# A wait on VectorE for GpSimd's next planned instruction, in an attention and mixture kernel

## The chip, the cores and the metric

The kernel runs on one core of a Trainium2 chip. The metric is the device time of one execution in microseconds (us). The engines are TensorE (PE in the rows; PEld is its weight load), VectorE (DVE), ScalarE (ACT), GpSimd (POOL) and SyncE (SP), which issues the DMAs.

## What is computed

Two stages, both over batch 4, sequence 768. The first is attention over 8 heads of 64 in which a query sees only keys of its own hash bucket (six signs of a projection); the second takes its output (4 x 768 x 512) as the input of a mixture of four causal attention experts, two of which are chosen for each row.

```
q_bits = (q @ proj > 0); k_bits = (k @ proj > 0)          # 6 bits -> bucket
scores = where(q_bucket == k_bucket, scale * q @ k^T, -1e9)
x = softmax(scores) @ v                                   # 8 heads -> 512 columns
logits = x @ w_gate; the two largest of 4 -> softmax -> w
for e in 4 experts:
    q, k, v = x @ wq[e], x @ wk[e], x @ wv[e]
    a = softmax(causal(scale * q @ k^T))
    out += w[e] * (a @ v @ wo[e])
```

## The kernel before

**Units.** The work is cut into 48 units: for each batch 8 heads of the first stage ("L") and 4 experts of the second ("M"). A unit first has a pass for its row maxima (matmuls into `mx`, reduced by VectorE into `pm`), then scores in chunks of up to 512 columns (matmuls into `st`, three PSUM buffers), and for each chunk two exponentials on ScalarE: `p` in float32 and `ph` in float16. GpSimd subtracts them: `pl = p - ph` is the low half, so that a product with float32 precision is made of float16 matmuls. `pl` has five buffers, `p` four. TensorE then adds three matmuls for each 128 columns into `o`: `vh,ph`, `vl,ph` and `vh,pl`. Some chunks are kept whole in float32 (`pf`, matmul `o<-vf,pf`). `vl` is the low half of v, made by GpSimd from `vf` and `vh` too.

**Preparing a pair of heads** (`prep_pair`). For two heads at a time `natq` and `natk` (float32, 128 x 768) are loaded, ScalarE makes the scaled float16 half (`qk<-natq,cs`), and VectorE the rest: `scalar_tensor_tensor` `qk<-natq,cs,qk`, an instruction that reads two SBUF operands. There are 14 such for q and 14 for k. Then follow projection matmuls into `misc`, the signs `M`, and DMAs (`qk<-M`, `qk<-qk`) that lay the rows out. In the last unit VectorE also takes five of the `pl` subtractions, the other instructions of it with two SBUF operands that last long.

**The order.** Nothing is issued as it is written. A recorder keeps every operation, and `schedule()` plans: from a table of durations (`TIMES`) and priorities (`prio`, with the table `PLACE`) it picks, step by step, the operation that can start first on any engine, and `issue()` emits them in that order. Each engine then runs its own list strictly in order, and waits on semaphores for what it reads or overwrites. For the planner, `port` marks VectorE's instructions with two SBUF operands; `hold` is the planned start and end of the last of these, `grain` the planned start and end of GpSimd's last instruction. The planner knows that the two do not overlap: a marked VectorE instruction that starts in the middle of a GpSimd one is given an end after it, and a GpSimd instruction planned within `hold` starts 130 ns before its end. But this is only arithmetic for the order. In the program nothing ties the two engines together there: which of them goes first is settled when it runs. All instructions are emitted by one line, so rows carry L711 throughout and are told apart by their tiles.

Of the kernel before, what the change touches and what calls it, by code (L numbers as in the profile page):

```python
# [42 lines left out]
class View:  # L43
# [42 lines left out]
    def real(self):  # L86
        x = self.tile.real
        for name, args, kw in self.path:
            x = getattr(x, name)(*args, **kw)
        return x  # L90
# [42 lines left out]

class Op:
    __slots__ = ("i", "alts", "ins", "outs", "preds", "succ", "wait", "ready", "new", "done", "prio", "wide", "dma",
                 "bias", "end", "eng", "tag", "job")


PRIO = {"norm": -300, "pair_scales": -100, "shift_steps": -100, "halves": 50, "mixture_scales": -3000, "weights": 400}
# [325 lines left out]
class Recorder:  # L465
# [102 lines left out]
    def schedule(self):  # L568
        groups = {}
        for o in self.ops:  # L570
            g = groups.setdefault((str(o.job), o.alts[0][0]), len(groups))
            o.prio = o.i + PRIO.get(o.tag, 0) + PRIO.get((o.tag, o.alts[0][0]), 0) + (PLACE[g] if PLACE else 0)
            o.wait, o.done, o.eng = len(o.preds), False, None
            for p in o.preds:
                p.succ.append(o)
        free = dict(START)
        cand = {e: [] for e in free}

        def sources(o, e):
            other = {p if p.eng == "sync" else p.eng for p in o.preds if p.eng != e}  # L580
            return len(other) > 1

        def after(p, e, many):
            if p.eng == e:
                return p.end + SAME[e]
            return p.end + (LAT_PE[e] if e in LAT_PE and many and p.eng == "tensor" else (LAT2 if many else LAT)[e])

        def enter(o):
            o.ready = {}
            for a in o.alts:  # L590
                e, r = a[0], 0.0
                many = sources(o, e)
                for p, over in o.preds.items():
                    if p.eng == e and (e == "tensor" or not over):
                        continue
                    r = max(r, after(p, e, many))
                o.ready[e] = r
                cand[e].append((o, a))

        for o in self.ops:  # L600
            if not o.wait:
                enter(o)
        order = []
        last = queue = 0.0
        grain = hold = (-1e9, -1e9)
        left = len(self.ops)
        while left:
            left -= 1
            best = None
            for e, lst in cand.items():  # L610
                t0 = free[e]
                k0 = k1 = 1e18
                pick = None
                for o, a in lst:
                    r = o.ready[e]
                    if max(t0, r) > k0:
                        continue
                    ok = True
                    for i, c in enumerate(o.new):
                        if not c.placed:  # L620
                            old = c.ring.ready(c, sum(d.ring is c.ring for d in o.new[:i]))
                            if old is None:
                                ok = False
                                break
                            if old:
                                for p in old.ops:
                                    if p.eng != e or e != "tensor":
                                        r = max(r, after(p, e, False))
                    if not ok:
                        continue  # L630
                    st = max(t0, r)
                    pen = max(0.0, 107.0 - last - max(0.0, st - t0)) if e == "tensor" and o.wide else 0.0
                    if a[4][4] and grain[1] > st + 187.0 and grain[0] + 80.0 < st:
                        pen = grain[1] - 187.0 - st
                    if len(o.alts) > 1 and a is o.alts[1]:
                        f = o.alts[0]
                        late = free[f[0]] + sum(p.alts[0][4][0] for p, _ in cand[f[0]] if p.prio < o.prio and p.ready[f[0]] <= st)
                        if max(late, r) + f[4][1] <= st + pen + a[4][1] - o.bias:
                            continue
                    k = st + pen  # L640
                    if k < k0 or (k == k0 and o.prio < k1):
                        k0, k1, pick = k, o.prio, (st, o, a, pen)
                if pick and (best is None or pick[0] < best[0]):
                    best = pick
            if best is None:
                raise RuntimeError("no instruction can go")
            st, o, a, pen = best
            e = a[0]
            busy, lasts, lands, shares, port = a[4]
            for x in o.alts:  # L650
                cand[x[0]] = [y for y in cand[x[0]] if y[0] is not o]
            if e == "tensor":
                st += pen if o.wide else 0.0
                last = busy
                if st < COLD and busy < 300:
                    busy *= 1.85
                if self.filler and self.filler[0].done:
                    gap = st - max(free[e], self.filler[2])
                    if any(c.name == "o" for c in o.new):
                        self.filler = None  # L660
                    elif st < FILL_END:
                        for _ in range(int(0.8 * (gap - FILL_GAP) / (107.0 if st < COLD else 55.0))):
                            order.append((self.filler[0], self.filler[1]))
            if o.dma is not None:
                free[e] = st + busy
                o.end = max(st + lasts + lands, queue + shares)
                queue = max(queue, o.end)
                o.end += LATE
            elif e == "gpsimd":
                if hold[1] - 130.0 > st and hold[0] < st + 80.0:  # L670
                    st = hold[1] - 130.0
                grain = (st, st + lasts)
                free[e], o.end = st + busy, st + lasts
            elif port:
                o.end = st + lasts
                if grain[1] > st + 187.0 and grain[0] + 80.0 < st:
                    o.end = max(o.end, grain[1] + lasts - 187.0)
                free[e] = o.end - (lasts - busy)
                hold = (st, o.end)
            else:  # L680
                free[e], o.end = st + busy, st + lasts
            o.eng = e
            for c in o.new:
                if not c.placed:
                    c.placed = True
                    c.ring.done.append(c)
                    c.ring.next += 1
            for c in {x.tile for x in o.ins + o.outs}:
                c.left -= 1
            o.done = True  # L690
            if self.filler and o is self.filler[0]:
                self.filler = (o, self.filler[1], o.end + 300.0)
            for p in o.succ:
                p.wait -= 1
                if not p.wait:
                    enter(p)
            order.append((o, a))
        self.length = max(o.end for o in self.ops)
        return order

    def issue(self):
        def real(x):
            if not isinstance(x, View):
                return x
            return x.real()

        for o, (e, m, args, kw, _) in self.schedule():
            for c in o.new:
                if c.real is None:
                    c.real = c.pool.tile(c.shape, c.dtype, name=c.name, bufs=c.bufs)  # L710
            getattr(getattr(self.nc, e), m)(*[real(x) for x in args], **{k: real(x) for k, x in kw.items()})  # L711

# [30 lines left out]
@with_exitstack  # L745
def tile_kernel(ctx, tc, q, k, v, proj, w_gate, wq, wk, wv, wo, out):
    nc = Recorder(tc.nc, loose=("misc",))
    B, HP, _, _, HS = q.shape
    E, Dm, D = wq.shape
    H, S = 2 * HP, 2 * HS  # L750
# [82 lines left out]
    for j in range(2):  # L833
        part = slice(D * j, D * j + D)
        for sign, c0, n in ((1.0, 32 * j, 70), (-1.0, 32 * j + NB, 58)):
            x = first[part, c0:c0 + 2 * n].rearrange("p (a b) -> p a b", a=2)[:, :, 0:NB]
# [4 lines left out]
    for g in range(4):  # L841
        o = 32 * g
# [19 lines left out]
    for j in range(2):  # L862
        part = slice(D * j, D * j + D)
        for sign, lo, hi in ((1.0, 0, 88), (-1.0, 2 * NB, 2 * NB + 40)):
            x = signed[part, lo:hi].rearrange("p (a b) -> p a b", a=2)[:, :, j:j + 2 * NB:2]
# [1019 lines left out]
```

## Time and profile before

| | us |
|---|---|
| median of 3 runs | 617.88 |
| lowest, highest | 616.58, 618.98 |
| the profiled execution, its own time | 618.62 |
| its span, first to last instruction | 616.8 |
| PE busy | 596.4 (97%) |
| DVE busy | 505.8 (82%) |
| ACT busy | 502.1 (81%) |
| POOL busy | 466.9 (76%) |
| mean granted TensorE clock | 0.986 |

Busy time counts an instruction from its start to its end as the profiler saw them, so an instruction that has started and stands still counts as busy. Matmuls overlap, so PE's share is of time in which at least one is under way. A granted clock of 1.00 is the 2.4 GHz level and 0.50 the 1.2 GHz level. In a row of the timeline the two numbers are start and duration in us; xN are N instructions in a row; the bracket is how long the engine had been idle before, and what ended that.

### The profile page before, as it was taken

What the parts mean: (1) busy time and instruction counts of PE and PEld (TensorE: products, weight loads), DVE (VectorE), ACT (ScalarE), POOL (GpSimd) and SP (SyncE); (2) the same over time, 40 slices, a digit from 0 to 9 for tenths busy, and PEclk for the clock granted to TensorE, in tenths of its full rate; (3) what the DMA queues carried; (4) which work ended last, traced back from release to release, by engine and by line L of the source; (5) the groups of instructions that cost most, each with busy time, mean ns of one, the idle gap of its engine ahead of it and who ended that gap; (6) DMA issues with size and microseconds to landing.
All of it is one profiled execution on the core that took longest, in us unless ns stands there. A gap on an engine that the chain in (4) does not pass through costs nothing.

```text
span 616.8 us, 20449 instructions
## 1 busy us (share of the span) xinstructions
PE 596.4 (97%) x7850; PEld 431.7 (70%) x7850; DVE 505.8 (82%) x1374; ACT 502.1 (81%) x1075; POOL 466.9 (76%) x520
## 2 busy tenths in 40 slices
PE   8999996999999999999999999999999999999997
PEld 6668874767677776777776666767766767777673
DVE  5897888899999899988989879895979884557753
ACT  6686995899979889886998798896987978953784
POOL 9476795799976889995897679886895878961640
PEclk9997997999999999999999999999999999999999
DMA  6552072233242113232233314132024121001222
GB/s 183 168 143 66 12 194 95 55 96 64 77 146 91 47 29 112 52 96 63 73 85 120 106 54 124 39 105 59 16 92 126 51 51 29 24 20 42 63 86 103
DMA packets 38967, 50.24 MB, mean 81 GB/s; under 512 B 13226, under 2 KB 27350, under 8 KB 38870
## 3 DMA queue, kind: packets, MB, share of 16 engines
q1 hardware_dynamic: 38870, 48.95, 27.9%
q8 instruction: 61, 1.00, 0.7%
q14 instruction: 36, 0.29, 0.2%
HBM read 20.98 MB, written 6.29 MB: 44 GB/s over the span
## 4 chain that ended last, share of the span: by engine, by line
PE 77%; DVE 9%; ACT 7%; POOL 2%; issue 2%; DMA 1%; SPq 1%; ACTq 0%; DVEq 0%; POOLq 0%
PE st L711 24%; PE misc L711 22%; PE o L711 19%; PE mx L711 12%; DVE qk L711 3%; DVE pm L711 3%; ACT ph L711 2%; ACT p L711 2%; DVE misc L711 1%; ACT wst L711 1%; SPq L711 1%; POOL qk L711 1%; ACT qk L711 1%; DMA wst<-in_moe_wk_dram 0%; DMA xt<-roww 0%
## 5 line engine op out<-in xcount | busy, mean ns | idle before, releaser
L711 POOL TENSOR_TENSOR pl<-p,ph 128x512 f16<-128x512 f32 x367 | 411.4, 1148 | 120.7 <-ACT ph L711 57.8
L711 ACT ACTIVATE p<-st 128x512 f32<-128x512 f32 x372 | 230.1, 623 | 32.0 <-PE st L711 25.8
L711 ACT ACTIVATE ph<-st 128x512 f16<-128x512 f32 x372 | 230.4, 629 | 1.0 <-PE o L711 0.8
L711 PE MATMUL st<-qk 78*128 78x512 f16 (+3 forms) x976 | 229.8, 326 | 0.9 <-DMA qk<-row 0.6
L711 DVE TENSOR_REDUCE pm<-mx 128x2 f32<-128x512 f32 (+2 forms) x284 | 186.9, 675 | 18.0 <-PE mx L711 16.7
L711 PEld LDWEIGHTS <-ph 128*128 128x128 f16 x2880 | 157.5, 98 | 26.1 <-issue 1.8
L711 PEld LDWEIGHTS <-qk 128*128 128x128 f16 (+5 forms) x1560 | 130.6, 98 | 58.3 <-issue 8.8
L711 PE MATMUL mx<-qk 76*128 76x512 f16 (+2 forms) x488 | 137.0, 328 | 7.1 <-DVE pm L711 6.4
L711 PEld LDWEIGHTS <-pl 128*128 128x128 f16 x1440 | 132.8, 97 | 7.8 <-POOL pl L711 1.7
L711 PE MATMUL o<-vh,ph 128*128 128x65 f16 (+1 forms) x1104 | 127.1, 195 | 2.4 <-DVE xp L711 0.9
L711 PE MATMUL o<-vl,ph 128*128 128x64 f16 x1104 | 126.6, 193 | 0.2 <-POOL vl L711 0.2
L711 PE MATMUL o<-vh,pl 128*128 128x65 f16 (+1 forms) x1104 | 125.4, 194 | 0.0
L711 PE MATMUL misc<-xt,wqk_h 128*128 128x384 f16 x256 | 57.7, 325 | 0.2 <-DVE qk L711 0.2
L711 DVE CUSTOM_DVE_ANT_0 spare<-mx,causal 128x512 bf16<-128x512 f32 (+2 forms) x96 | 44.3, 461 | 9.2 <-PE mx L711 7.4
L711 PEld LDWEIGHTS <-xt 128*128 128x128 f16 x324 | 30.3, 97 | 10.8 <-ACT xt L711 0.5
L711 PE MATMUL o<-mvh,pl 128*128 128x65 f16 x336 | 37.2, 193 | 0.6 <-POOL pl L711 0.6
L711 PE MATMUL o<-mvh,ph 128*128 128x65 f16 x336 | 37.5, 194 | 0.0
L711 PE MATMUL o<-mvl,ph 128*128 128x64 f16 x336 | 37.4, 192 | 0.0
L711 POOL TENSOR_TENSOR vl<-vf,vh 128x384 f16<-128x384 f32 x32 | 30.6, 967 | 7.8 <-ACT vh L711 7.8
L711 PEld LDWEIGHTS <-wqk_h 128*128 128x128 f16 x256 | 24.1, 98 | 14.6 <-issue 0.3
L711 ACT ACTIVATE qk<-misc 128x384 f16<-128x384 f32 x26 | 13.2, 507 | 20.3 <-PE misc L711 20.1
L711 PE MATMUL misc<-wvg_h,xt 128*128 128x260 f16 x192 | 29.7, 274 | 0.0
(198 smaller groups left out, 911.3 us busy)
## 6 DMA issues: line engine op xcount, KB each, us to landing
qk<-qk SPq DMA_DIRECT2D x128, 96.0 KB
natv<-in_v_dram SPq DMA_DIRECT2D x16, 384.0 KB
qk<-qk SPq DMA_DIRECT2D x32, 192.0 KB
natq<-in_q_dram SPq DMA_DIRECT2D x15, 384.0 KB
natk<-in_k_dram SPq DMA_DIRECT2D x15, 384.0 KB
out_dram<-ot SPq DMA_DIRECT2D x20, 256.0 KB
xt<-xt SPq DMA_DIRECT2D x4, 192.0 KB
out_dram<-p SPq DMA_DIRECT2D x3, 256.0 KB
```

Source lines behind the costliest of these rows:

```text
L711: getattr(getattr(self.nc, e), m)(*[real(x) for x in args], **{k: real(x) for k, x in kw.items()})
```

## The change

In the planner, each VectorE instruction with two SBUF operands that lasts 400 ns or more by the table is remembered (`half`). The next GpSimd instruction whose planned start lies more than 100 ns after that instruction's start gets it as `after`, and when it is emitted a semaphore wait on that VectorE instruction is added to it. If a second such VectorE instruction is planned before any GpSimd instruction qualifies, it takes the place of the first, so that one wait stands for both. The plan's times, the ranks and so the order are not touched.

```diff
@@ schedule()
-            o.wait, o.done, o.eng = len(o.preds), False, None
+            o.wait, o.done, o.eng, o.after = len(o.preds), False, None, None
...
         grain = hold = (-1e9, -1e9)
+        half = None
...
             elif e == "gpsimd":
+                if half is not None and hold[0] + 100.0 < st:
+                    o.after, half = half, None
                 if hold[1] - 130.0 > st and hold[0] < st + 80.0:
                     st = hold[1] - 130.0
...
                 hold = (st, o.end)
+                if lasts >= 400.0:
+                    half = o
...
@@ issue()
-            getattr(getattr(self.nc, e), m)(*[real(x) for x in args], **{k: real(x) for k, x in kw.items()})
+            o.made = getattr(getattr(self.nc, e), m)(*[real(x) for x in args], **{k: real(x) for k, x in kw.items()})
+            if o.after is not None:
+                self.tc.add_manual_dep(o.made.ins, o.after.made.ins.name,
+                                       mybir.DependencyInfo(mybir.DependencyClass.Sync, mybir.DependencyReason.DATA), reason="port")
@@ tile_kernel()
     nc = Recorder(tc.nc, loose=("misc",))
+    nc.tc = tc
```

The program has 33 VectorE instructions that are remembered (28 `qk` and 5 `pl`) and gets 25 waits, all on GpSimd: 18 on `pl` of the units before the last, 5 on `vl`, 1 on `wvg_l` (a weight's low half) and 1 on the `pl` that GpSimd keeps in the last unit. The lists of TensorE, VectorE, ScalarE and SyncE are the same as before, word for word.

The first place is the third of the 14 pairs that are prepared this way, 94 us into the span. VectorE's list there, before and now (the two `qk` residuals stand one behind the other, so one wait serves both, and it is on the second):

```order
L711 TENSOR_REDUCE qkmax<-wst 128x2 [waits DMAHW3_49,DMAHW0_49]
L711 TENSOR_TENSOR xp<-o,rden 128x6x64 [waits DVE_49]
L711 TENSOR_REDUCE qkmax<-wst 128x2 [waits DMAHW2_49,DMAHW1_49]
L711 SCALAR_TENSOR_TENSOR qk<-natq,cs_1846,qk 128x2x384 [waits Activation_49]
L711 SCALAR_TENSOR_TENSOR qk<-natk,cs_1846,qk 128x2x384 [waits Activation_49,Pool_49]
L711 TENSOR_REDUCE pm_177<-mx 128x2 x2
L711 TENSOR_REDUCE qkmax<-wst 128x2 [waits DMAHW5_49,DMAHW4_49]
```

Nothing moved in it: the reductions `pm` that free the two `mx` buffers for TensorE are queued behind both residuals (`qkmax` is the largest entry of a weight in `wst`). GpSimd's list at 94 us, before (numbers behind `p` are buffer names):

```order
L711 TENSOR_TENSOR pl<-p_1949,ph 128x512 [waits PE_49,Activation_49,Pool_49]
L711 TENSOR_TENSOR pl<-p_1981,ph 128x512 [waits PE_49,Activation_49,Pool_49]
L711 TENSOR_TENSOR vl_939<-vf_259,vh_253 128x6x64 x2
L711 TENSOR_TENSOR pl<-p_2054,ph 128x512 [waits PE_49,Activation_49,Pool_49]
L711 TENSOR_TENSOR pl<-p_2094,ph 128x512 [waits PE_49,Activation_49,Pool_49]
L711 TENSOR_TENSOR pl<-p_2111,ph 128x512 [waits PE_49,Activation_49,Pool_49]
```

and with the change:

```order
L716 TENSOR_TENSOR pl<-p_1949,ph 128x512 [waits PE_49,Activation_49,Pool_49]
L716 TENSOR_TENSOR pl<-p_1981,ph 128x512 [waits PE_49,Activation_49,Pool_49]
L716 TENSOR_TENSOR vl_939<-vf_259,vh_253 128x6x64 x2
L716 TENSOR_TENSOR pl<-p_2054,ph 128x512 [waits PE_49,DVE_49,Activation_49,Pool_49]
L716 TENSOR_TENSOR pl<-p_2094,ph 128x512 [waits PE_49,Activation_49,Pool_49]
L716 TENSOR_TENSOR pl<-p_2111,ph 128x512 [waits PE_49,Activation_49,Pool_49]
```

No row has moved; the first `pl` behind the two `vl` has one more semaphore to wait for, VectorE's, and what is queued behind it on GpSimd waits with it. The second place is the pair at 332 us, on GpSimd before:

```order
L711 TENSOR_TENSOR vl_939<-vf_259,vh_253 128x6x64 [waits Activation_49]
L711 TENSOR_TENSOR pl<-p_7524,ph 128x256 [waits PE_49,Pool_49]
L711 TENSOR_TENSOR pl<-p_7657,ph 128x512 [waits PE_49,Activation_49,Pool_49]
L711 TENSOR_TENSOR pl<-p_7685,ph 128x512 [waits PE_49,Activation_49,Pool_49]
L711 TENSOR_TENSOR pl<-p_7757,ph 128x512 [waits PE_49,Activation_49,Pool_49]
```

and with the change:

```order
L716 TENSOR_TENSOR vl_939<-vf_259,vh_253 128x6x64 [waits DVE_49]
L716 TENSOR_TENSOR pl<-p_7524,ph 128x256 [waits DVE_49,PE_49,Pool_49]
L716 TENSOR_TENSOR pl<-p_7657,ph 128x512 [waits PE_49,Activation_49,Pool_49]
L716 TENSOR_TENSOR pl<-p_7685,ph 128x512 [waits PE_49,Activation_49,Pool_49]
L716 TENSOR_TENSOR pl<-p_7757,ph 128x512 [waits PE_49,Activation_49,Pool_49]
```

Here the second `vl` waits for the residual of q and the `pl` behind it for that of k: two waits on two instructions that follow each other.

## Rows read from the trace of the kernel before

**Rows 1.** The page: busy time of each engine; the chain by engine.

```profile
PE 596.4 (97%) x7850; PEld 431.7 (70%) x7850; DVE 505.8 (82%) x1374; ACT 502.1 (81%) x1075; POOL 466.9 (76%) x520
...
PE 77%; DVE 9%; ACT 7%; POOL 2%; issue 2%; DMA 1%; SPq 1%; ACTq 0%; DVEq 0%; POOLq 0%
```

**Rows 2.** Timeline of PE, 90 to 112 us: start, duration, instruction, idle before.

```profile
96.25 0.33 PE L711 MATMUL misc<-qk,pbl 128*32 128x384 f16 x3
101.56 0.59 PE L711 MATMUL mx<-qk 76*128 76x512 f16 x1 [4.97 <-DVE pm L711]
...
107.35 0.24 PE L711 MATMUL o<-vh,pl 128*128 128x65 f16 x1
```

**Rows 3.** Timeline of DVE, 90 to 108 us.

```profile
93.93 6.04 DVE L711 SCALAR_TENSOR_TENSOR qk<-natq,cs,qk 128x768 f16<-128x768 f32 x1
99.89 1.00 DVE L711 SCALAR_TENSOR_TENSOR qk<-natk,cs,qk 128x768 f16<-128x768 f32 x1
100.82 1.28 DVE L711 TENSOR_REDUCE pm<-mx 128x2 f32<-128x512 f32 x2
```

**Rows 4.** Timeline of POOL, 75 to 108 us.

```profile
74.71 4.12 POOL L711 TENSOR_TENSOR pl<-p,ph 128x512 f16<-128x512 f32 x3
...
92.88 1.83 POOL L711 TENSOR_TENSOR vl<-vf,vh 128x384 f16<-128x384 f32 x2
94.66 4.50 POOL L711 TENSOR_TENSOR pl<-p,ph 128x512 f16<-128x512 f32 x4
104.01 0.92 POOL L711 TENSOR_TENSOR vl<-vf,vh 128x384 f16<-128x384 f32 x1 [4.86 <-ACT vh L711]
```

**Rows 5.** Stretches: length; busy PE, PEld, DVE, ACT, POOL; granted clock; DMA.

```profile
85.00:95.00 10.00, 9.12 (x137) 7.01 (x134) 9.78 (x27) 9.64 (x20) 10.00 (x11) 1.00 0.76 169
95.00:100.60 5.60, 1.58 (x33) 1.03 (x32) 5.60 (x2) 2.34 (x6) 4.15 (x4) 1.00 0.62 214
100.60:110.80 10.20, 9.24 (x55) 5.55 (x55) 7.75 (x13) 4.66 (x10) 3.19 (x3) 0.50 0.11 27
...
110.80:122.00 11.20, 10.91 (x182) 8.73 (x181) 9.58 (x34) 11.05 (x23) 8.78 (x8) 1.00 0.20 46
```

**Rows 6.** Timeline of ACT, 88 to 112 us.

```profile
102.39 0.27 ACT L711 ACTIVATE vr<-misc 1x128 f16<-1x128 f32 x1 [5.05 <-PE misc L711]
...
103.41 0.53 ACT L711 ACTIVATE vh<-vf 128x384 f16<-128x384 f32 x1
105.76 0.62 ACT L711 ACTIVATE vf<-natv,cs 128x384 f32<-128x384 f32 x1 [1.83 <-PE o L711]
...
110.12 0.60 ACT L711 ACTIVATE p<-st 128x512 f32<-128x512 f32 x1 [1.79 <-PE st L711]
```

**Rows 7.** Tile natq: the residuals of q; least, median, most ns.

```profile
L711 DVE SCALAR_TENSOR_TENSOR qk<-natq,cs,qk x14: 996/1015/6045, 35.2 to 480.6; 128x768 f16<-128x768 f32 x14
```

**Rows 8.** Timeline of DVE at four other residuals.

```profile
75.57 1.11 DVE L711 SCALAR_TENSOR_TENSOR qk<-natk,cs,qk 128x768 f16<-128x768 f32 x1
...
155.29 2.14 DVE L711 SCALAR_TENSOR_TENSOR qk<-natq,cs,qk 128x768 f16<-128x768 f32 x1 [0.57 <-ACT qk L711]
...
196.87 1.76 DVE L711 SCALAR_TENSOR_TENSOR qk<-natk,cs,qk 128x768 f16<-128x768 f32 x1
...
331.81 2.14 DVE L711 SCALAR_TENSOR_TENSOR qk<-natq,cs,qk 128x768 f16<-128x768 f32 x1
```

**Rows 9.** Tile pl: the subtraction on POOL; who waited for it (us, times).

```profile
L711 POOL TENSOR_TENSOR pl<-p,ph x367: 664/1155/1882, 22.1 to 601.7; 128x512 f16<-128x512 f32 x169, 128x384 f16<-128x384 f32 x15
...
  PEld L711: 1.7, 6
```

**Rows 10.** Timeline of PE: its idle time behind three of those residuals.

```profile
159.60 0.38 PE L711 MATMUL mx<-qk 76*128 76x512 f16 x1 [0.26 <-DVE pm L711]
...
199.64 0.23 PE L711 MATMUL misc<-identh,negh 128*128 128x128 f16 x1 [0.58 <-DVE negh L711]
...
337.86 0.23 PE L711 MATMUL misc<-identh,negh 128*128 128x128 f16 x1 [0.66 <-DVE negh L711]
```

More of the change, by code (lines that the diff above doesn't have):

```diff
@@ L135 @@
     __slots__ = ("i", "alts", "ins", "outs", "preds", "succ", "wait", "ready", "new", "done", "prio", "wide", "dma",
-                 "bias", "end", "eng", "tag", "job")
+                 "bias", "end", "eng", "tag", "job", "after", "made")
 PRIO = {"norm": -300, "pair_scales": -100, "shift_steps": -100, "halves": 50, "mixture_scales": -3000, "weights": 400}
```

## The prediction

> **What bounds the kernel now.** I read the page first, then PE's idle time, then what stood before it on the other engines. By the page PE has work under way for 97% of the span and is most of the chain [rows 1]: there is little idle time to win, so the question is where the little is, and what the clock did there. Of PE's idle pieces one stands out: 4.97 us, ended by VectorE's `pm`, before the matmul into `mx` at 101.56 us [rows 2]. The last instruction before it started at 96.25 (a row of three, so PE went idle at 101.56 - 4.97 = 96.6).
>
> VectorE was not idle. The residual of q started at 93.93 and took 6.04 us, that of k followed at 99.89, and the `pm` behind them came only at 100.82 [rows 3]. The same residual takes 1.015 us in the median of its 14 calls, and 6.045 at most [rows 7]. So about 5.0 us of the 6.04 are standing still. What it stood still for is seen on GpSimd: at 93.93 it was in the second of two `vl`, and then ran four `pl` without a gap, up to 94.66 + 4.50 = 99.16 [rows 4]. The residual ended 0.81 us after that, when GpSimd had nothing more to run. Both read two operands from SBUF; the residual stood through the rest of that `vl` and was passed over by four `pl` in a row.
>
> The stretch after it shows a second cost. From 100.6 to 110.8 PE is busy for 9.24 of 10.20 us at a granted clock of 0.50, the 1.2 GHz level; in the stretches before and after it is 1.00 [rows 5]. PE had been idle for 4 us, from 96.6, when it fell. That is the place where this change has something to win.
>
> **The change part by part.**
>
> *The wait at 94 us.* The first `pl` behind the two `vl` now waits for the residual of k. GpSimd can then get no further than the second `vl`, which ends at 92.88 + 1.83 = 94.71 [rows 4]. The residual of q runs from about there and ends near 95.6, that of k 0.93 later (the steps of [rows 3]: 100.82 - 99.89) near 96.5, and the first `pm`, half of a row of two that takes 1.28, some 0.6 later at 97.1. Before, this was at 101.5. PE resumes 4.45 us earlier, and 0.5 us of its idle time stays.
>
> *The clock.* With an idle piece of 0.5 us I expect 1.00 to stay: from 85 to 95 us PE was busy for 9.12 of 10.00, so idle for 0.9, and the clock held [rows 5]. PE's 9.24 us at half speed would then need 4.62 at the least, 4.62 less. PE alone therefore allows 4.45 + 4.62 = 9.05 us.
>
> *Who is next.* ACT is busy for 11.05 of 11.20 us in the stretch after that [rows 5], so no more comes through than ACT loses of its idle time. That was 5.05 + 1.83 + 1.79 = 8.67 us [rows 6]. Scaled: `vr` starts 0.83 us after PE resumes (102.39 - 101.56), at full clock 0.42, so near 97.5, where ACT had been free since 102.39 - 5.05 = 97.34: 0.2 us stays. `vf` at 105.76 came 4.2 after PE, so 2.1 now, and ACT is through `vh` (103.41 + 0.53) about as late: 0.2 stays. Before 110.12 nothing stays, since PE halves its 8.56 us and ACT's own work of 2.56 does not shrink. ACT allows 8.2. VectorE: 4.4 earlier at the end of the residuals, and its idle time from 100.6 to 122 is 2.45 + 1.62 = 4.07 [rows 5], 8.5 together, of which it must win nearly all. Three engines near their limit don't all win all of it. I take 7.5 for this place, nearest to ACT, with 4.45 (clock stays low, or other engines eat it) and 9.05 as ends.
>
> *The other waits.* Three more residuals lost a turn or more to GpSimd: 2.14, 1.76 and 2.14 us [rows 8] against 1.01; with the wait they would be through some 0.6 to 0.9 earlier (one `wvg_l`, one `vl` that comes after). PE stood idle behind them for 0.26, 0.58 and 0.66 [rows 10], 1.5 in all; half of it is my estimate, 0.7.
>
> *What the waits cost on GpSimd.* At 94 us the `pl` starts when the residual of k has ended and been seen, 96.5 + 0.07 (the handover from ACT's `vh`, 103.94, to `vl` at 104.01 [rows 4, 6]) instead of 94.66: 1.9 us of idle time on an engine that was busy for 10.00 of 10.00 us before [rows 5]. Behind it are three more `pl`. What covers it: the first of them is used at 107.35 [rows 2], 11.5 us after its end at 95.8; even with PE 9 us earlier that is 2.5 of margin against 1.9. At the three other lost turns the guarded instruction comes about 1 us later. At nine waits GpSimd's instruction was already standing and started as VectorE let go (the longest `pl`, 1882 ns against a median of 1155 [rows 9]); to see one: the three `pl` from 74.71 end at 78.83 [rows 4], the second so at about 77.7, 1.0 after the residual of 75.57 + 1.11 [rows 8]; for one that takes 1.155 that is a start 0.13 before the residual's end, and with a semaphore it is some 0.07 after: 0.2 each. At the other eleven it began after the residual's end anyway, among them the `pl` of the last unit: nothing. Almost all of this is covered, because PE waits for `pl` only six times in the whole run, 1.7 us together [rows 9]. Bounds: 0 and 9 x 0.2 + 3 = 4.8 if all of it came through; I take 0.4, near the first, for that row. The added semaphore checks themselves I put at nothing: they stand in GpSimd's idle quarter [rows 1].
>
> **Sum.** 7.5 + 0.7 - 0.4 = 7.8 us. The profiled execution took 618.62, 0.74 above the median of 617.88: 610.8 on its scale, 610.1 on the median's.
>
> **A rule against it.** The row at 93.93 shows a residual passed over by four GpSimd instructions [rows 3, 4]; the one at 75.57, which also came in the middle of a `pl`, took 1.11, so it was next [rows 8]. The Trainium skill (SBUF — State Buffer, section "Who interferes with whom") says of the port pair that these two engines share: "Whoever issues first gets the shared pair for the whole instruction; the other fully blocks." By it a residual stands for the rest of one GpSimd instruction and then has its turn, and a wait would have nothing to win. The row at 75.57 agrees, that at 93.93 doesn't. By that rule the sum would be -0.4 instead of 7.8, and the time 618.3.
>
> **The rivals.** *Nothing to win* (that mechanism): the residual at 93.93 is normally next, and the 6.04 us belong to this one execution, or the loss turns up at another residual, where two or more GpSimd instructions stand between it and the wait (the pair at 128 us has two `pl` before the guarded one). Time 617.9 + 0.4 = 618.3. Against it: the profiled execution, with the loss, lies inside the three timed ones (616.58 to 618.98), which agree within 0.4% where the loss is worth over 1%. Chance 0.10.
>
> *The clock falls all the same*, or VectorE and ACT hold PE to the old pace: 4.45 + 0.3 is won, 613.1. For it: VectorE is busy for 7.75 of 10.20 us in that stretch [rows 5], and at twice PE's pace has no room. Against it: much of VectorE's work there can run on into the time after, where it had 1.62 us idle [rows 5]. Chance 0.14; faster still.
>
> *Slower*: GpSimd waits for a VectorE that is late. The place is a stretch where GpSimd has no gap, as 85 to 95 us with 10.00 of 10.00 [rows 5]. There a wait for a residual that comes d later than GpSimd's turn puts all `pl` behind it back by d, and once d is over the margin of `pl` and over the 4 us in which the clock held here, PE pays what it paid at 101 us: 4.97 + 4.62 = 9.6. By this trace's times no guarded instruction would be held for more than the 1.9 us above, so it decides from some 4 us of lateness, and takes two such places to lose more than is won: 618.6 - 7.8 + 2 x 9.6 = 630, 629 on the median's scale. Chance 0.04.
>
> **How the numbers follow.** The forecast has 0.72, the clock rival 0.14, nothing to win 0.10, slower 0.04. About 0.5%, 3.1 us, is what a measurement of this kernel can tell from no change: faster means under 614.8. Forecast and clock rival lie there: faster 0.86, same 0.10, slower 0.04. The range goes from all bounds at their best, 617.9 - 9.05 - 1.5 = 607.3, to the clock rival with the costs at their higher side, 617.9 - 4.45 + 1.5 = 615.0. Likeliest 610.1.
>
> **What would show it.** Right: the residual of q near 94 us takes about 1.6 us; PE's idle piece there is under 1 us; the clock stays at 1.00 from 95 to 111; no residual over 2 us in the natq and natk views; GpSimd shows 1.9 us idle, ended by VectorE's `qk`, and a `pl` that no one misses. VectorE's busy time falls by 6 to 8 us without an instruction less. Wrong: the 6 us residual comes up at another pair, the clock falls near 100 us without a long idle piece, or PE waits for `pl` far more than 1.7 us.

## The result, and the profile after

The changed kernel took 609.54 us in the median of 4 runs (608.91 to 610.19). The kernel before, run beside it, took 617.23 (615.38 to 618.98). The ratio is 0.9876, with an interval of 0.9844 to 0.9908: 1.2% faster. Its profiled execution took 609.53 us, with a span of 607.8 and a mean granted clock of 0.994 (before: 618.62, 616.8 and 0.986).

The page after, busy time and chain by engine (answers to [rows 1]), and between them the TensorE clock granted, in tenths, over 40 slices:

```profile
PE 593.4 (98%) x7850; PEld 429.4 (71%) x7850; DVE 499.0 (82%) x1374; ACT 502.1 (83%) x1075; POOL 463.1 (76%) x520
...
PEclk9997999999999999999999999999999999999999
...
PE 83%; DVE 6%; ACT 5%; DMA 2%; issue 2%; POOL 1%; SPq 1%; ACTq 0%; POOLq 0%; DVEq 0%
```

The same line of before:

```profile
PEclk9997997999999999999999999999999999999999
```

Not an instruction more or less, yet VectorE is busy for 6.8 us less (505.8 to 499.0): that is standing time which had counted as work, 4.97 us of it at 94 us. Of the two dips of the clock before, in the fourth and the seventh slice, the second is gone. In the chain VectorE has 6% instead of 9%.

The place itself. Timeline of VectorE after (answers to [rows 3]; start, duration, instruction):

```profile
95.21 1.07 DVE L716 SCALAR_TENSOR_TENSOR qk<-natq,cs,qk 128x768 f16<-128x768 f32 x1
96.21 1.01 DVE L716 SCALAR_TENSOR_TENSOR qk<-natk,cs,qk 128x768 f16<-128x768 f32 x1
97.13 1.28 DVE L716 TENSOR_REDUCE pm<-mx 128x2 f32<-128x512 f32 x2
```

Timeline of GpSimd after ([rows 4]):

```profile
93.67 1.80 POOL L716 TENSOR_TENSOR vl<-vf,vh 128x384 f16<-128x384 f32 x2
97.38 4.51 POOL L716 TENSOR_TENSOR pl<-p,ph 128x512 f16<-128x512 f32 x4 [1.92 <-DVE qk L716]
```

Timeline of PE after ([rows 2]); no bracket stands at `mx` any more:

```profile
97.60 0.33 PE L716 MATMUL misc<-qk,pbl 128*32 128x384 f16 x3
97.87 0.39 PE L716 MATMUL mx<-qk 76*128 76x512 f16 x1
```

The residual of q comes while the second `vl` runs, as before, and is next: 1.07 us instead of 6.04. The four `pl` wait 1.92 us, and the bracket says for whom. PE goes from the projection into `mx` without a pause, where it had stood for 4.97 us. The stretches after (columns as in [rows 5], same bounds):

```profile
95.00:100.60 5.60, 5.60 (x93) 4.01 (x90) 5.60 (x10) 5.25 (x13) 3.68 (x4) 1.00 0.69 229
100.60:110.80 10.20, 10.01 (x171) 7.82 (x169) 9.95 (x30) 10.20 (x22) 10.20 (x11) 1.00 0.29 69
```

From 100.6 to 110.8 the clock is now 1.00 instead of 0.50, and PE, VectorE, ACT and GpSimd are all busy for nearly the whole stretch.

**Where the 9.0 us of span went.** PE's list is the same in both kernels, so one matmul can be found in both traces. Two of them fence the place in: the row of three `misc<-qk,pbl` ahead of it, and the first `misc<-identh,negh` behind it. Before, the first starts at 96.25 [rows 2] and the second here:

```profile
117.92 0.22 PE L711 MATMUL misc<-identh,negh 128*128 128x128 f16 x1
```

After:

```profile
110.13 0.22 PE L716 MATMUL misc<-identh,negh 128*128 128x128 f16 x1
```

Between the two lie 117.92 - 96.25 = 21.67 us before, and 110.13 - 97.60 = 12.53 after: the place gave 9.14 us. Of that 4.97 is PE's idle time; the other 4.17 is put down to PE's work running at 1.00 instead of 0.50, which `pe_busy` below tests. Ahead of the place the execution after is 1.35 us late (97.60 against 96.25), and behind it, up to the end of the span, it takes 607.8 - 110.13 = 497.7 instead of 616.8 - 117.92 = 498.9, 1.2 less. So 1.35 - 9.14 - 1.2 = -9.0. The same three sums of the profiled execution of every kernel below (us, one execution each):

| kernel | waits | ahead of the place | place | rest |
|---|---|---|---|---|
| before | none | 96.25 | 21.67 | 498.9 |
| after | all 25 | 97.60 | 12.53 | 497.7 |
| `again` (the changed kernel) | all 25 | 96.32 | 12.75 | 497.2 |
| `only94` | the one at 94 us | 97.45 | 12.94 | 498.4 |
| `five` | five | 98.13 | 13.21 | 496.8 |
| `but94` | all but the one at 94 us | 96.99 | 20.55 | 497.7 |
| `stall5` | all, VectorE held up by 4.89 | 95.56 | 21.45 | 498.2 |
| `stall2` | all, VectorE held up by 1.93 | 95.69 | 17.34 | 497.9 |
| `pe_busy` | none, PE given work | 96.38 | 17.46 | 500.7 |
| `nudge` | none, residual later by one reduction | 96.67 | 20.71 | 500.5 |
| `nudge2` | none, later by two | 96.38 | 21.90 | 499.8 |
| `write_only` | none, four `pl` only write | 93.49 | 13.20 | 498.0 |

The column of the place is what this change is about, and free of what happens by chance elsewhere: ahead of it the executions differ by up to 4.6 us, for the most part with the time that they spend early on at half clock (none in `write_only`, 3.4 us in four of them, 6.8 in six, 13.7 in `five`).

### The profile page after: what moved, and what is told of

Same layout as the page of the kernel before. It is cut to its first block, busy times and chain, and to the rows that moved or that the text cites. A ratio compares the mean times of both kernels' runs of the same rounds, so it can differ in the third digit from the quotient of the medians.

```text
span 607.8 us, 20469 instructions
## 1 busy us (share of the span) xinstructions
PE 593.4 (98%) x7850; PEld 429.4 (71%) x7850; DVE 499.0 (82%) x1374; ACT 502.1 (83%) x1075; POOL 463.1 (76%) x520
## 4 chain that ended last, share of the span: by engine, by line
PE 83%; DVE 6%; ACT 5%; DMA 2%; issue 2%; POOL 1%; SPq 1%; ACTq 0%; POOLq 0%; DVEq 0%
PE misc L716 25%; PE st L716 25%; PE o L716 21%; PE mx L716 13%; ACT ph L716 2%; DVE pm L716 1%; ACT p L716 1%; DMA natv<-in_v_dram 1%; POOL pl L716 1%; DVE qk L716 1%; DVE xt L716 1%; SPq L716 1%; DMA wst<-in_moe_wk_dram 1%; DVE misc L716 1%; DMA xt<-roww 0%
## 5 line engine op out<-in xcount | busy, mean ns | idle before, releaser
L716 ACT ACTIVATE p<-st 128x512 f32<-128x512 f32 x372 | 227.7, 616 | 30.2 <-PE st L716 24.2
L716 ACT ACTIVATE ph<-st 128x512 f16<-128x512 f32 x372 | 228.0, 621 | 0.6 <-PE o L716 0.4
L716 PE MATMUL mx<-qk 76*128 76x512 f16 (+2 forms) x488 | 135.6, 325 | 1.9 <-DVE pm L716 1.0
L716 POOL TENSOR_TENSOR vl<-vf,vh 128x384 f16<-128x384 f32 x32 | 29.3, 925 | 6.0 <-DVE qk L716 2.6
```

The source lines that it names most:

```text
L716: o.made = getattr(getattr(self.nc, e), m)(*[real(x) for x in args], **{k: real(x) for k, x in kw.items()})
```

## The experiments

`n` counts the instructions that each engine is given, as they are issued; GpSimd's 143 is the first `pl` behind the two `vl`, VectorE's 180 the residual of q that stood for 6.04 us.

**One wait alone, and all but that one** (`only94`, `but94`).

```diff
@@ issue()
...
+            n = at[e] = at.get(e, -1) + 1
+            if e == "gpsimd" and not (n == 143):
+                o.after = None
```

So every wait is dropped but that of instruction 143; `but94` has `n != 143` there.

> Of the 25 waits one is kept, on the first pl behind the two vl at 94 us. Theory A (one place pays): the residual there takes 1.0 to 1.6 us, PE's 4.97 us idle piece shrinks under 1 us, the clock stays at 1.00 from 95 to 111 us, time 609.5 to 611.5. Rival B (the gain is the sum of many small ones at the other lost turns): under half of the gain, 614 or more.

> The 24 other waits are kept, the one at 94 us is left out. Theory A: the residual there takes about 6 us again, PE idles about 5 us, the clock falls to 0.50 for about 10 us; only the small gain of the other places is left, time 616 to 617.5. Rival B: half of the gain or more, 613 or less.

With the one wait: 610.3 us (607.84 to 610.57) against 618.12 of before, ratio 0.9866 (0.9800 to 0.9931). The residual took 1.50 us, and the place 12.94. Its row in VectorE's timeline, the matmul behind it in PE's, and a stretch (columns of [rows 5]):

```profile
95.06 1.50 DVE L721 SCALAR_TENSOR_TENSOR qk<-natq,cs,qk 128x768 f16<-128x768 f32 x1
```

```profile
98.15 0.38 PE L721 MATMUL mx<-qk 76*128 76x512 f16 x1 [0.36 <-DVE pm L721]
```

```profile
99.00:106.00 7.00, 6.90 (x90) 5.11 (x90) 7.00 (x15) 6.63 (x14) 7.00 (x7) 1.00 0.28 90
```

With the 24 others the profiled execution has the loss again (place 20.55 us), timelines of VectorE, GpSimd and PE:

```profile
94.59 6.20 DVE L721 SCALAR_TENSOR_TENSOR qk<-natq,cs,qk 128x768 f16<-128x768 f32 x1
```

```profile
95.49 4.49 POOL L721 TENSOR_TENSOR pl<-p,ph 128x512 f16<-128x512 f32 x4
```

```profile
102.38 0.58 PE L721 MATMUL mx<-qk 76*128 76x512 f16 x1 [5.05 <-DVE pm L721]
```

But its ten times fall in two groups: 616.22 to 618.08 five times, and 607.12 to 610.67 five times, so its median (613.44), which lies between what the two theories expected, says little. Nor is the kernel before of one kind: of its 25 runs beside these two, five took 611.64 to 613.30, and the rest 615.38 to 619.72; beside the next kernels one of 19 was that low (611.94), and none of 13 beside the last. None of the 16 runs of the kernels with the wait at 94 us and nothing added was over 611. So it is one place and one wait that bring nearly all. The likely reading of the two groups is that whether the residual is passed over is settled anew in each execution: in most of before's it is, in about half of those of `but94`. This is not shown, since none of the low executions was profiled; in all five profiled executions without this wait (before, `but94`, `pe_busy`, `nudge`, `nudge2`) it was passed over.

**The same lateness without the passing over** (`stall5`, `stall2`). All waits stay, and VectorE is given 5 or 2 reductions that read one SBUF operand, ahead of the residual. GpSimd is then late as well, since its `pl` waits for the residuals, but PE's pause is ended by VectorE's `pm`, as before.

```diff
@@ issue()
...
+            if e == "vector" and n == 180:
+                out, src = self.idle
+                out.tile.real = out.tile.pool.tile(out.tile.shape, out.tile.dtype, name="idle", bufs=1)
+                for _ in range(5):
+                    self.nc.vector.tensor_reduce(out.real(), src.real(), axis=AX.XY, op=OP.max)
```

`stall2` has `range(2)`.

> All 25 waits, and VectorE gets five reductions of 768 elements (each about 0.95 us, one SBUF operand, into a tile that nobody reads) right ahead of the residual of q at 94 us: the same hold-up of VectorE without any passing over. Theory A (what costs is that VectorE comes about 5 us late to the pm behind it: PE's idle time and then the clock): PE idles about 5 us, the clock falls, time 616 to 618. If only the contention itself cost, or ScalarE and GpSimd set the pace: under 612. If the idle time counts but the clock holds: 613 to 614.5.

> As the one with five reductions, with two, about 1.9 us. Theory A: PE idles 2 to 2.5 us, the clock holds at 1.00, and the time is 1.5 to 2 us over the changed kernel, 611 to 611.5. If the clock fell for this too: 614 to 616. If VectorE has slack there: 609.5.

`stall5`: 617.02 us, ratio 1.0003 (0.9963 to 1.0042). VectorE timeline, PE timeline, and a stretch in the columns of [rows 5]:

```profile
93.17 4.89 DVE L723 TENSOR_REDUCE idle<-ident 128x1 f32<-128x768 f32 x5
97.98 1.01 DVE L724 SCALAR_TENSOR_TENSOR qk<-natq,cs,qk 128x768 f16<-128x768 f32 x1
```

```profile
100.57 0.58 PE L724 MATMUL mx<-qk 76*128 76x512 f16 x1 [4.68 <-DVE pm L724]
```

```profile
99.00:106.00 7.00, 5.43 (x25) 3.25 (x25) 5.36 (x9) 2.64 (x6) 5.38 (x5) 0.55 0.02 4
```

A residual that takes its 1.01 us, but 4.9 us late, costs what the one that stood cost: place 21.45 us against 21.67. So the price is that VectorE comes late, with the clock behind it, and the standing adds nothing that can be seen.

`stall2`: 612.72 us (611.18 to 616.25), ratio 0.993 (0.9894 to 0.9966). Timeline of PE, and two stretches:

```profile
97.73 0.38 PE L724 MATMUL mx<-qk 76*128 76x512 f16 x1 [1.71 <-DVE pm L724]
```

```profile
99.00:106.00 7.00, 7.00 (x47) 4.71 (x46) 5.44 (x9) 4.24 (x9) 5.86 (x6) 0.52 0.14 34
106.00:111.00 5.00, 4.91 (x81) 3.65 (x79) 3.83 (x12) 4.72 (x11) 3.95 (x4) 0.99 0.42 95
```

I had expected the clock to hold with so short a pause. It fell to the 1.2 GHz level all the same, behind the pause, while PE was busy for 7.00 of the 7.00 us. The place took 17.34 us, 4.8 more than after, for 1.93 us of delay: 1.71 in PE's idle time, the other 3.1 with the clock. The median is only 2.4 us above that of `only94`, which ran beside it (612.72 against 610.3), so other executions seem to have paid less; one was profiled.

**The clock's part by itself** (`pe_busy`). No waits; 72 short matmuls, whose result nobody reads, fill PE's idle piece ahead of `mx` (`seen` is the number of VectorE's last instruction issued).

```diff
@@ issue()
...
+            if e == "tensor" and o.outs[0].tile.name == "mx" and o.tag == "max" and seen >= 182 and not put:
+                put = True
+                spot = next(x for x, a in seq[k + 1:] if a[0] == "tensor").outs[0].tile.real[:, 384:512]
+                for _ in range(72):
+                    self.nc.tensor.matmul(spot, self.small.real(), self.small.real(), start=True, stop=True)
```

> No wait at all, as before, but TensorE gets 72 extra matmuls (128 columns, into columns of a PSUM tile that nobody reads) right ahead of the matmul into mx that waits about 5 us: some 4 us of work in place of idle time. It parts the clock from the idle time. If the fall of the clock is half of the loss (theory A): the clock stays at 1.00 from 95 to 111 us and the time is 613 to 615, with or without the passing over, since the extra work delays the mx matmul either way. If ScalarE and VectorE set the pace there and the clock costs nothing: 616 to 619.

615.4 us (613.24 to 617.80) against 618.26, ratio 0.9973 (0.9944 to 1.0001). Timelines of VectorE and PE, a stretch, and the matmul behind the place:

```profile
94.39 5.63 DVE L728 SCALAR_TENSOR_TENSOR qk<-natq,cs,qk 128x768 f16<-128x768 f32 x1
```

```profile
96.65 4.19 PE L727 MATMUL misc<-ident 128*128 128x128 bf16 x72
101.60 0.38 PE L728 MATMUL mx<-qk 76*128 76x512 f16 x1 [0.76 <-DVE pm L728]
...
113.84 0.22 PE L728 MATMUL misc<-identh,negh 128*128 128x128 f16 x1
```

```profile
99.00:106.00 7.00, 6.24 (x85) 4.79 (x83) 7.00 (x12) 3.44 (x8) 1.44 (x3) 1.00 0.02 8
```

The residual still stands (5.63 us) and `mx` comes as late (101.60 against 101.56), but the clock stays at 1.00, and the place takes 113.84 - 96.38 = 17.46 us: 4.21 less than before. That agrees with the 4.17 that were left over above. The other way round: `mx` comes 4.95 us later behind the row of three than after the change (101.60 - 96.38 against 97.87 - 97.60), and the place takes 4.93 more. With the clock held, lateness costs itself and no more. The times alone would not show it: in the medians it is 2.9 us, just outside the 613 to 615 that I expected, and the interval of the ratio reaches 1.0001. The profiled execution took 1.8 us longer than before's behind the place, so a part of the difference is given away elsewhere.

**What decides who is next** (`nudge`, `nudge2`). No waits (`not (False)` drops them all); one or two of the reductions of `stall5` ahead of the residual, so that it should meet a `pl` instead of the second `vl`.

```diff
@@ issue()
...
+            if e == "gpsimd" and not (False):
+                o.after = None
+            if e == "vector" and n == 180:
...
+                for _ in range(1):
+                    self.nc.vector.tensor_reduce(out.real(), src.real(), axis=AX.XY, op=OP.max)
```

`nudge2` has `range(2)`.

> No wait at all, as before, but VectorE gets one reduction of 768 elements (about 0.95 us, one SBUF operand) ahead of the residual of q at 94 us, so that it comes while GpSimd runs a pl and not the second vl. If it matters which instruction it meets (in the trace of before all residuals that met a pl were next, those that met a vl or a wvg_l were not): residual at most 2 us, PE idle under 2 us, time 611 to 613.5 in nearly every execution. If it is chance whenever GpSimd runs without a gap: 616 to 619 in half of the executions or more, as before.

> No wait, as before, and two reductions (about 1.9 us) ahead of the residual of q at 94 us, so that it comes in the middle of the first pl; with one it had still met the last 0.26 us of the second vl and was passed over by all four pl. If it matters what it meets: the residual is next behind that pl and takes at most 2 us, the pm behind it comes about 3 us late instead of 4.5, time 612 to 615 without a group at 617. If GpSimd without a gap passes it over whatever it meets: the residual ends about 0.8 us after the last pl again, near 100 us, and the time is 616 to 619 as before.

`nudge`: 616.74 us (615.39 to 620.49), ratio 0.9981 (0.9958 to 1.0005). The shift was too small to tell: the residual began at 95.14, with 0.2 us of the `vl` still to go (the `pl` follow at 95.34), and took 5.53. Its clock is needed below; PE was idle from 97.00 to 102.25 us there:

```profile
99.00:106.00 7.00, 3.75 (x17) 2.11 (x17) 6.54 (x10) 1.42 (x3) 1.78 (x2) 0.50 0.07 27
```

`nudge2`: 617.43 us, ratio 0.9996 (0.9971 to 1.0021). Timelines of VectorE and GpSimd:

```profile
95.86 4.36 DVE L726 SCALAR_TENSOR_TENSOR qk<-natq,cs,qk 128x768 f16<-128x768 f32 x1
```

```profile
94.92 4.49 POOL L726 TENSOR_TENSOR pl<-p,ph 128x512 f16<-128x512 f32 x4
```

Here it came 0.94 us into the first `pl`, and was passed over by the three that followed. So the `vl` is not what makes it lose. What does decide isn't settled: at 75.57 us a residual that met a `pl` was next [rows 8], here it was not. It is no blind chance everywhere: in the four profiled executions of the full program without waits (before, `pe_busy`, `nudge`, `nudge2`) each of the 27 other residuals takes the same to within 0.2 us.

**Which five, and the changed kernel again** (`five`, `again`). `five` keeps the wait at 94 us and four at the three other pairs of [rows 8].

```diff
@@ issue()
...
+            if e == "gpsimd" and not (n in (143, 189, 219, 327, 328)):
+                o.after = None
```

> Of the 25 waits the five are kept that stand behind a lost turn in the trace of before (at 94, 155, 197, and two at 332 us). If the other 20 only cost GpSimd 0.2 us here and there under cover: the same as the changed kernel within 0.5 us, 609 to 610.5. If they win something too: 611 or more.

> The changed kernel beside the others on the same chip: 609 to 610.5, with no execution near 617.

608.02 us (607.29 to 609.89), ratio 0.9834 (0.9801 to 0.9867), and 608.09 (606.40 to 610.60), ratio 0.9843 (0.9799 to 0.9888). Both are about 1 us below what I expected, and the same as each other. The other 20 waits neither win nor cost anything that can be measured.

**Is it what GpSimd reads?** (`write_only`). No waits; the four `pl` are replaced by instructions that only write (the kernel leaves out the low halves of four chunks).

```diff
@@ issue()
...
+            if e == "gpsimd" and 143 <= n <= 146:
+                m, args, kw = "memset", (args[0], 0.0), {}
```

> No wait, as before, but the four pl that passed the residual at 94 us by are memsets of the same tiles, which read nothing from SBUF (the low halves of four chunks are left out). If GpSimd's reads are what the residual stands for: it ends 0.8 us after the second vl, takes 1.0 to 1.8 us, PE idles under 1 us, time 609 to 612. If any GpSimd instruction passes it by: it ends 0.8 us after the fourth memset, about 3 to 3.5 us, time 612 to 615.

609.72 us (606.44 to 611.15), ratio 0.9893 (0.9860 to 0.9925). Timelines of VectorE and GpSimd:

```profile
91.10 1.78 DVE L723 SCALAR_TENSOR_TENSOR qk<-natq,cs,qk 128x768 f16<-128x768 f32 x1
92.80 1.01 DVE L723 SCALAR_TENSOR_TENSOR qk<-natk,cs,qk 128x768 f16<-128x768 f32 x1
```

```profile
90.25 1.80 POOL L723 TENSOR_TENSOR vl<-vf,vh 128x384 f16<-128x384 f32 x2
92.00 1.91 POOL L723 MEMSET pl<- 128x512 f16 x4
```

The residual stands up to the end of the second `vl` (90.25 + 1.80 = 92.05), and ends 0.83 us later, at 92.88, while the memsets run: its own work, done beside them. The residual of k behind it runs from 92.80 to 93.81, all of it beside the memsets (92.00 to 93.91), and takes its usual 1.01 us. There is nothing left to wait for, and the place takes 13.20 us without any wait. What the memsets lack against the four `pl` is the reads of SBUF; they are also shorter, but they were under way for the whole of both pieces. So it is the reads that the residual stands for.

## Why the prediction was right, and where its steps were off

**The mechanism was right.** The 6.04 us were standing time behind a `vl` and four `pl`; a wait on the first of these `pl` removes it (`only94`), and the time falls with it. Most signs named ahead came: the residual near 94 us took 1.07 us (I had put 1.6), no PE idle piece is left there, the clock stays at 1.00 from 95 to 111, GpSimd shows 1.92 us ended by VectorE's `qk`, VectorE's busy time fell by 6.8, and no residual is over 2 us. One did not: a `pl` that no one misses (see the cost on GpSimd). Tiles natq and natk after (least, median, most in ns; answers to [rows 7]):

```profile
L716 DVE SCALAR_TENSOR_TENSOR qk<-natq,cs,qk x14: 1001/1030/1798, 36.0 to 471.5; 128x768 f16<-128x768 f32 x14
```

```profile
L716 DVE SCALAR_TENSOR_TENSOR qk<-natk,cs,qk x14: 999/1070/1911, 37.7 to 474.1; 128x768 f16<-128x768 f32 x14
```

**The place was taken too small: 7.5, measured 9.14** (8.92 in `again`, 8.73 in `only94`). It lies at the upper end that I had drawn, 4.45 + 4.62 = 9.05. The two parts were each about right: the idle time gave 4.97, since all of it went and not all but 0.5, and the clock gave 4.17 to 4.21 of at most 4.62. The step that failed is the cut from 9.05 to 7.5, "three engines near their limit don't all win all of it". ACT's idle time there did go almost whole, as the sum by ACT said; timeline of ACT after ([rows 6]):

```profile
98.56 0.25 ACT L716 ACTIVATE vr<-misc 1x128 f16<-1x128 f32 x1
...
100.25 0.62 ACT L716 ACTIVATE vf<-natv,cs 128x384 f32<-128x384 f32 x1 [0.30 <-PE o L716]
```

Of 8.67 us 0.30 stays. VectorE, ACT and GpSimd kept up with PE's full pace there (two of them busy for 10.20 of 10.20 us), so next to nothing was to be charged for their being near their limit.

**The other waits: 0.7 less 0.4 of costs, measured 1.2** behind the place (498.9 to 497.7; 1.7 in `again`). The kernels with these waits take 496.8 to 498.2 us there, those without 498.0 to 500.7, one profile each. So some 1 us is likely theirs, but the bounds overlap. It fits that the three idle pieces of PE [rows 10] are still there in `only94` (0.27, 0.57 and 0.68 us) and gone in `five`: the whole of the 1.5 and not half of it. Of the three lost turns one is won back whole, one mostly and one by a third (the longest residual left, 1.91 us, is that of k in the pair at 128 us, which takes 1.91 before as well); timeline of VectorE after ([rows 8]):

```profile
147.51 1.80 DVE L716 SCALAR_TENSOR_TENSOR qk<-natq,cs,qk 128x768 f16<-128x768 f32 x1 [0.57 <-ACT qk L716]
...
189.04 1.01 DVE L716 SCALAR_TENSOR_TENSOR qk<-natk,cs,qk 128x768 f16<-128x768 f32 x1
...
323.84 1.38 DVE L716 SCALAR_TENSOR_TENSOR qk<-natq,cs,qk 128x768 f16<-128x768 f32 x1
```

The three idle pieces behind them are gone here too.

**The cost on GpSimd** is seen, and not quite covered. Tile pl after ([rows 9]):

```profile
L716 POOL TENSOR_TENSOR pl<-p,ph x367: 667/1155/1875, 22.9 to 592.6; 128x512 f16<-128x512 f32 x169, 128x384 f16<-128x384 f32 x15
...
  DVE qk L716: 10.9, 6
...
  PEld L716: 4.2, 13
```

GpSimd waits for `qk` ahead of six `pl`, 10.9 us in all, and PE's weight loads wait for `pl` 4.2 us, 13 times, where it was 1.7, 6 times. That is 2.5 more than before and more than the 0.4 that I charged, and of the signs of being wrong it is the one that came nearest. 1.0 of it is the price of the wait at 94 us: two weight loads wait for `pl` right behind the place, 0.59 us at 111.53 and 0.42 at 112.65, and in `again`, `only94` and `five` two do so as well, in before none. PE's matmul there:

```profile
111.54 0.20 PE L716 MATMUL o<-vh,pl 128*128 128x66 f16 x1 [0.29 <-POOL pl L716]
```

The margin of 2.5 us was reckoned for the first `pl` behind the wait. But GpSimd has no gap from 97.38 to 112.55 us, so the 1.92 us by which it starts late are handed on to the `pl` at the end of that row. PE itself stands for only 0.29 of it, and the rest doesn't come through to the end: behind the place the changed kernel is not longer than before, and one wait, five and 25 give ratios whose intervals overlap (0.9866, 0.9834, 0.9843).

**That the total fits** is in part luck. The steps add up to 9.14 + 1.2 = 10.3 us, not 7.8; the profiled execution lost 1.35 ahead of the place, where the executions differ by more than that among themselves. `again`, which came to the place as early as before (96.32), gained the whole: 616.8 to 606.3 in span, 10.5 us. In the medians it is 7.7 us in the first comparison and 10.2 in the second, so the 7.8 of the forecast stands at the lower end.

**The rivals.** *Nothing to win* was dismissed by a wrong argument. I took three runs within 0.4% for a loss that is in every execution. In before's 57 other runs beside the experiments, six were as low as 611.6 to 613.3, and I read these as executions without the loss or with a part of it: for them there is little to win. *The clock falls all the same* was nearer than I thought. I had the clock hold through 4 us without PE; `stall2` shows it at half behind a pause of 1.71, and in `nudge` it was at 0.50 by 99.00, 2.0 us into the pause at the latest. In `but94` it held longer, for some 4.8 us: over the same 7 us it has a mean of 0.72, which leaves 3.9 us at half, from about 102.1, where PE had been idle since 97.33. So the 4 us were one execution's, not a margin. In `stall2` VectorE came 1.9 us later, and half of the gain was gone (place 17.34 instead of 12.53, 4.8 of 9.14). *Slower* rests on the same point, "over the 4 us in which the clock held": 1.93 us of lateness were enough to lose the clock in `stall2`. The waits of the change themselves left no such pause.

**The rule against it.** The trace had spoken both ways, and the runs do too. By the Trainium skill (SBUF — State Buffer, section "Who interferes with whom") a VectorE instruction with two SBUF inputs contends with a GpSimd instruction that reads SBUF, not with one that only writes it. `write_only` agrees: 0.83 us beside four memsets. That whoever issues first holds the ports for one instruction explains the standing behind the `vl`; it does not explain the four `pl` that started while the residual stood.

**What stays open:** what decides, between a residual that stands and GpSimd's next instruction, who goes first; and why the low runs of `but94` (607 to 611) lie some 2 us below the low runs of before (611.6 to 613.3). The latter take what `stall2` takes (612.72), where the loss is there in part, so there the residual may have been passed over by fewer `pl`; no trace shows it.

## What to carry to other kernels

Where one instruction of a shape takes several times its median, look at what the other engines ran beside it: here 5 us of standing for another engine's reads were counted as busy time, and no wait was shown for them. An order that two engines are only assumed to keep can be made certain with one semaphore, put on the engine whose results are wanted later, at the one place where both queues are full; here 1.9 us of GpSimd's time bought 9 of PE's, and PE gave 0.3 back. Follow that engine's delay up to its next gap, not only up to the first instruction behind the wait. And compare whole sets of runs before a loss in one profile is taken for a loss in all.

## What the runs showed of the hardware that was not expected

A VectorE instruction that stands for GpSimd's reads was passed over by three or four GpSimd instructions in a row (4.36 to 6.20 us instead of 1.01), while another one of the same shape, in the same execution, was next (1.11 us). That it differs from one execution of the same program to the next is read from the times alone.

Behind a single PE pause of 1.71 us the granted clock was at the 1.2 GHz level for most of the next 7 us (a mean of 0.52, `stall2`), and a delay of 1.93 us cost 4.8 at that place; it held at 1.00 with a pause of 0.36 (`only94`) and one of 0.76 (`pe_busy`). In pauses of about 5 us it fell after under 2.0 us (`nudge`), 4.0 (before) and some 4.8 (`but94`).

The early dip of the clock, in the fourth slice of both pages, differs between executions: it is absent in `write_only`, which is the kernel before up to that place and whose mean clock is 1.000, and there the place is reached at 93.49 us instead of 96.25. One of the four runs of `only94` has a mean clock of 1.000 too, and 607.84 us against 610.07 to 610.57 of the others, at 0.993.
